# Linear attention behind an adaptive layer norm: the numerators' low parts taken by VectorE straight from the PSUM banks

## The chip, the cores and the metric

The kernel runs on one core of a Trainium2 chip. The metric is the device time of one execution in microseconds (us). The engines are named as in the profile: PE is TensorE (PEld its weight loads), DVE is VectorE, ACT is ScalarE, POOL is GpSimd, SP is the engine whose queue issues most DMAs. A bank is one of the eight 128 x 512 fp32 buffers of PSUM, into which TensorE writes its products.

## The reference

The block takes x (2048 x 640) and a condition vector. Its first half is the attention:

```python
q, k, v = qkv[0], qkv[1], qkv[2]                   # 32 heads of 20
pq = einsum("bhsd,hdf->bhsf", q, w_phi); pk = einsum("bhsd,hdf->bhsf", k, w_phi)
phi_q = concat([softmax(pq), softmax(-pq)]); phi_k = concat([softmax(pk), softmax(-pk)])
kv = einsum("bhsf,bhsd->bhfd", phi_k, v);  z = einsum("bhsf->bhf", phi_k)
num = einsum("bhqf,bhfd->bhqd", phi_q, kv)
den = einsum("bhqf,bhf->bhq", phi_q, z)[..., None] + 1e-6
x = x + ga * ((num / den) @ wo)
```

It is followed by a second modulated layer norm and a two-layer MLP with squared ReLU (640 to 1728 to 640). The change lies in the attention, between num and the product with wo.

## The kernel before, in words

The 2048 rows are 16 tiles of 128, worked on as 8 pairs of tiles. To keep fp32 accuracy, TensorE multiplies in a reduced format (fp32r): each operand is split into a high part (a rounded copy) and a low part (the value less the high part), and a product is three products, high x high, high x low, low x high (`three`). A low part is usually made by `lo`, a VectorE subtraction.

There are three stages. From 0 to about 250 us: the modulation, q, k, v and the sum kv over all rows. From about 250 to 394 us: the attention's tail, where the change lies. From 394 us to the end: the MLP.

Before the tail the exponentials of q are written to DRAM for the first 12 tiles (esp) and read back as el; the last four tiles (12 to 15, `KEPT` = 12) stay on chip, and those of tiles 13, 14, 15 are still made inside the tail: `q_chain` (max, min and two subtractions on VectorE, 13, 14, 15 in j = 1, 3, 5), `exps` (ScalarE), `q_sums` (VectorE). For each tile t the tail then does:

- `e_prod(t)`: VectorE multiplies by z and sums by head (L869, L871); POOL makes the small denominators (L874 to L878).
- `e_recip(t)`, `e_scale(t)`: VectorE inverts them and scales the exponentials; the result is e' (tile ezb, L893 and L898).

For each pair j of tiles:

- `tr_e(j, groups)`: TensorE turns e' by a product with the identity, in six groups of heads (tile te, L913), ScalarE copies each bank out (ept, L915, L917).
- `num(j)`: TensorE multiplies with the block diagonal kv into three banks numa, numb and numc. The first two are used over 512 columns each; numc holds two parts of 256 columns side by side.
- `num_hi(j)`: ScalarE copies the four parts to the high parts of ot (L942).
- `num_lo(j)`: the low parts. TensorE adds minus the identity times the high part into the same banks (L948), so that the bank then holds the low part, and ScalarE copies it out (L951).
- `do_wo(j, i, h, a, b)`: 16 products with wo for tile i of the pair and column block h (384 or 256 columns), tile pwo; ScalarE copies the result to at, and a DMA on its queue writes it to DRAM.

The loop over j runs these skewed: while TensorE does wo of pair j it turns and multiplies pair j + 1, and VectorE makes e' of tiles 2j + 4 and 2j + 5 and the denominators of 2j + 5 and 2j + 6. Each of PE, DVE, ACT and POOL works in the order in which the Python code issues its instructions, since the stage is under a manual schedule; SP's order is set by a planner. In every turn TensorE's order is: wo of tile 2j in two column blocks, wo of tile 2j + 1, first block, with the groups of `tr_e(j + 1)` in between; `num(j + 1)`; 11 products of the last block; the four products with minus identity; the last 5 products. `te_at` says behind which block the two groups of turns stand; for j = 0 (`late_te`) all six stand in one piece ahead of `num(1)`.

The banks of te, numa and numb come from one pool of three that goes round; numc has a bank of its own.

Of the kernel before, what the change touches and what calls it, by code (L numbers as in the profile page):

```python
# [15 lines left out]
P = 128  # L16
# [9 lines left out]
GR = [(120 * g, 120) for g in range(5)] + [(600, 40)]  # L26
NG = len(GR)
# [8 lines left out]
KEPT = NT - POSTPONED  # L36
W2_AT = 48
PLAIN = 2
LAST = 3
W_AT = (  # L40
    *range(21),
# [9 lines left out]
def kernel(  # L51
# [34 lines left out]
    def lo(out_lo, full, hi, eng=None):  # L86
        (eng or nc.vector).tensor_tensor(out_lo, full, hi.bitcast(F32), op=ALU.subtract)  # L87
# [377 lines left out]
    def q_chain(t, whole=True):  # L465
        if t < KEPT:
            EQ[t] = tok2(f"q{t % 2}", f"eq{t}")
        e = EQ[t]
        spread(PQ[t], e, f"q{t}")
        if whole:  # L470
            exps(e)
            q_sums(t)
# [238 lines left out]
    for t in range(2, NT - 2):  # L711
        j, i = divmod(t, 2)
# [167 lines left out]
    def e_recip(t):  # L880
        if t >= NT:
            return
        rs = rs_q[:, t].rearrange("p (s h) -> p s h", s=2)
        nc.vector.reciprocal(DD[t], DD[t])
        for s in range(2):
            nc.vector.tensor_tensor(DN[t][:, s], rs[:, 1 - s], DD[t], op=ALU.mult)

    def e_scale(t):
        if t >= NT:
            return  # L890
        dn = DN[t]
        EU[t] = EZB[t % 4]
        nc.vector.tensor_tensor(  # L893
            EU[t][:, :1200].rearrange("p (u s h d) -> p s u h d", s=2, h=3, d=DH),
            ET[t][:, :, :600].rearrange("p s (u h d) -> p s u h d", h=3, d=DH),
            dn[:, :, :30].rearrange("p s (u h) -> p s u h", h=3)[:, :, :, :, None].to_broadcast([P, 2, 10, 3, DH]), op=ALU.mult
        )
        nc.vector.tensor_tensor(  # L898
            EU[t][:, 1200:].rearrange("p (s h d) -> p s h d", s=2, d=DH),
            ET[t][:, :, 600:].rearrange("p s (h d) -> p s h d", d=DH),  # L900
            dn[:, :, 30:, None].to_broadcast([P, 2, 2, DH]), op=ALU.mult
        )

    def tr_e(j, gs):
        for g in gs:
            o, n = GR[g]
            p = bank(f"te{j}_{g}")
            t = EPT[j, g] = feat("s4", f"ept{j}_{g}")
            for i in range(2):
                for c in range(2 if g < 5 else 1):  # L910
                    a = c * 256 + i * P
                    b, m = (2 * o + 120 * c, 120) if g < 5 else (1200, 80)
                    nc.tensor.transpose(p[:m, a : a + P], EU[2 * j + i][:, b : b + m], ident)  # L913
            if g < 5:
                nc.scalar.activation(t[:120], p[:120].rearrange("p (s n) -> p s n", s=2), AF.Copy)  # L915
            else:
                nc.scalar.activation(t[:80, 0], p[:80, :256], AF.Copy)  # L917
# [15 lines left out]
    def num_parts(j):  # L933
        ps, parts = NUM[j], []
        for b, g in ((0, 2), (1, 2), (2, 1)):
            t = OT[j][:, 2 * b : 2 * b + g]
            parts.append((ps[b][:, : 256 * g].rearrange("p (g n) -> p g n", n=256), t[:, :, 0], t[:, :, 1]))
        return parts + [(ps[2][:120, 256:], OT[j, 5][:120], OT[j, 5][:120])]
# [4 lines left out]

    def num_lo(j):

        for b, (src, hi, _) in enumerate(num_parts(j)):
            r = 120 if b == 3 else P
            nc.tensor.matmul(src, neg[:r, :r], hi, start=False, stop=True, skip_group_check=True)  # L948
        for b, (src, _, low) in enumerate(num_parts(j)):
            r = GR[5][1] if b == 3 else P  # L950
            nc.scalar.activation(low[:r], src[:r], AF.Copy)  # L951
# [3 lines left out]
    def do_wo(j, i, h, a=0, b=16):  # L955
        t = 2 * j + i
        if h == 0 and a == 0:
            PWO[t] = pj(f"pwo{t}")
            AT[t] = row("s2", f"at{t}")
        s = slice(i * P, (i + 1) * P)  # L960
        cs_, n = slice(*CUT[h]), CUT[h][1] - CUT[h][0]
        terms = []
        for g in range(5):
            w, o = WO[g], OT[j]
            terms += three(o[:, g, 0, s], o[:, g, 1, s], w[:, 0, cs_], w[:, 1, cs_])
        terms.append((OT[j, 5][:120, s], WO[5][:120, 0, cs_]))
        mm(PWO[t][h][:, :n], terms[a:b], first=(a == 0), last=(b == 16))
        if b == 16:
            nc.scalar.activation(AT[t][:, cs_], PWO[t][h][:, :n], AF.Copy)
            if h:  # L970
                nc.scalar.dma_start(A1[t], AT[t])
# [83 lines left out]
    def load_xx(j):  # L1055
        if j:
            XX[j] = [row("s2" if j <= PLAIN else "s1", f"xx{j}_{i}") for i in range(2)]
        else:
# [62 lines left out]
    SPREAD, SUMS = {1: 1, 3: 2}, {2: 1, 4: 2}  # L1121
    ln0 = None
    for j in range(NB):
        nxt = j + 1 < NB
        b, c = 2 * j + 5, 2 * j + 6
        late_te = j == 0
        te_at = (0, 1) if 0 < j < 6 else (1, 2)
        if j == 4:
            load_x1(0)
        if j < 5:  # L1130
            p_load()
        if j != 5:
            e_prod(b)
        e_recip(b - 1)
        e_scale(b - 1)
        if j == 5:
            q_chain(KEPT + 3, False)
            add_x(0, 0, 1)
            nc.vector.tensor_tensor(bb, b2s[0], gb_b, op=ALU.mult)
            ln0 = ln_parts(XM[0], "b0")  # L1140
        load_e(b + 2)
        def te(at):
            for i, gs in enumerate((range(3), range(3, NG))):
                if nxt and not late_te and te_at[i] == at:
                    tr_e(j + 1, gs)

        do_wo(j, 0, 0)
        te(0)
        if j == 5:
            exps(EQ[KEPT + 3])  # L1150
            q_sums(KEPT + 3)
            e_prod(b)
        do_wo(j, 0, 1)
        if j == 7:
            t2(0, 0)
            t2(0, 1)
        te(1)
        if j == 5 or j == 6:
            next(ln0)
        if j in SUMS:  # L1160
            q_sums(KEPT + SUMS[j])
        e_prod(c)
        e_recip(b)
        e_scale(b)
        if j in SPREAD:
            q_chain(KEPT + SPREAD[j], False)
        do_wo(j, 1, 0)
        if j == 7:
            t2(0, 2)
            t2(0, 3)  # L1170
        te(2)
        if nxt:
            if late_te:
                tr_e(j + 1, range(NG))
            num(j + 1)
            num_hi(j + 1)
        do_wo(j, 1, 1, 0, 8)
        if j == 7:
            t2(0, 4)
        if not nxt:  # L1180
            do_wo(j, 1, 1, 8, 16)
        if nxt:
            do_wo(j, 1, 1, 8, 11)
            num_lo(j + 1)
            do_wo(j, 1, 1, 11, 16)
        if j in SPREAD:
            exps(EQ[KEPT + SPREAD[j]])
        load_e(c + 2)
        if j == 5:
            next(ln0)  # L1190
        if 1 <= j < 6:
            p_hi()
        if j == 5:
            p_lo(4)
            p_load(4)
        if j == 6:
            p_hi(4)
            p_lo(5)
            p_load(3)
        if j == 7:  # L1200
            p_load(2)
# [16 lines left out]
    def up(j, f):  # L1218

        n, k = FS[f], f % 2  # L1220
        p = UP2[:, :256] if k and j < PLAIN else UP[:, 256 * k : 256 * k + 256]
        terms = []
        for d in range(NC):
            if n == P:
                terms += three(W1[f][:, 0, d], W1[f][:, 1, d], H2[j][:, d, 0], H2[j][:, d, 1])
            else:
                terms += [(W1[f][:, 0, d], H2[j][:, d, 0]), (W1[f][:, 0, d], H2[j][:, d, 1])]
        mm(p, terms, first=(k == 0 or j < PLAIN), skip=True)
        if k == 0:
# [13 lines left out]
    def plain(j, n):  # L1243
        return j < PLAIN or n == NF // 2 - 1 or j == NB - 1 and n >= NF // 2 - LAST

# [6 lines left out]
    def split_a(j, n, parts=(0, 1)):  # L1252
        t = FT[j, n]
        if 0 in parts:
            tag = "rs" if j < PLAIN and (NP * j + n) % 2 or (j, n) == (NB - 1, NP - 1) else "ra"
            RA[j, n] = p3.tile([P, 2, 4, P], F32, tag=tag, name=f"ra{j}_{n}").bitcast(F32R)
# [27 lines left out]
    TD = [{r: dram.tile([P, 2, m], F32, name=f"td{n}_{r}") for r, m in RINGS.items()} for n in range(NP - 1)]  # L1284
    ITEMS = [(j, n, r) for j in range(PLAIN, NB) for n in range(NP) if not plain(j, n) for r in RINGS]
    L, R = slice(0, 384), slice(384, 640)
# [88 lines left out]
    def down_pair(j, n, part):  # L1375
        v, w = W2[2 * n], W2[2 * n + 1]
        last = n == (NF // 2 - 2 if j < NB - 1 else NF // 2 - 1 - LAST)
        if part:
# [127 lines left out]
    for j in range(NB):  # L1506
# [5 lines left out]
        for n in range(NP):  # L1512
# [46 lines left out]
            if j == NB - 1 and n == 1:  # L1559
                for k in range(NP - LAST, NP - 1):  # L1560
                    plain_load(k)
            if j == NB - 1 and n == 3:
                for k in range(NP - LAST, NP - 1):
                    plain_split(k)
# [100 lines left out]
```

## Time and profile before

| | us |
|---|---|
| median of 3 runs | 773.87 (773.56 to 774.21) |
| the profiled execution | 773.97 |
| its span, first to last instruction | 772.2 |
| PE busy | 764.6 (99%) |
| DVE busy | 580.3 (75%) |
| ACT busy | 443.3 (57%) |
| POOL busy | 145.5 (19%) |
| 276 to 394.4 us: PE, DVE, ACT busy | 118.30, 88.58, 75.53 of 118.40 |

A line of the order of time has its start, its duration, the engine, the line of the kernel, the operation, the tile written and the tiles read, the shapes and how many instructions are merged in it; in brackets how long the engine stood idle before it and what ended that. A line of the groups has the busy time, then the mean duration of one in ns, then the idle time before. A line of the stretches has, for each engine, its busy microseconds and in brackets its instructions, then TensorE's granted clock, the share of the DMA engines and GB/s. Durations of consecutive instructions on VectorE and ScalarE overlap by some tens of ns, so what one instruction costs its engine is the distance of starts.

### The profile page before, as it was taken

The numbers are of one execution on the slowest core, as the hardware profiler recorded it, in microseconds if no ns is written. First come the engines' busy times: TensorE is split into PE (matmuls) and PEld (weight loads), VectorE is DVE, ScalarE is ACT, GpSimd is POOL, SyncE is SP. The second block draws the span as 40 slices with busy tenths as digits, with TensorE's granted clock in tenths as the row PEclk, the third lists the DMA queues.
The fourth block names the chain that finished last, engine by engine and source line by source line (L and its number), as shares of the span: only waits on it lengthen the run. The fifth ranks groups of instructions, "written<-read, shape, count | busy, mean of one in ns | idle before, by whom it ended". The sixth has DMA issues, their size and how long they took to land.

```text
span 772.2 us, 15334 instructions
## 1 busy us (share of the span) xinstructions
PE 764.6 (99%) x5989; PEld 744.1 (96%) x5989; DVE 580.3 (75%) x1057; ACT 443.3 (57%) x995; POOL 145.5 (19%) x301
## 2 busy tenths in 40 slices
PE   9999999999999999999999999999999999999997
PEld 9999999999999979998999999999999999999997
DVE  6598897968999899976266666767767566685666
ACT  5766756667853355656776647456463645546331
POOL 3001101202000255631001001122221313213110
PEclk9999999999999999999999999999999999999999
DMA  9711431512333354232247465997666758667460
GB/s 332 297 65 73 137 103 54 186 37 101 133 103 109 111 160 157 86 105 101 91 137 251 137 212 215 292 320 234 202 178 213 231 178 264 198 185 208 128 171 35
DMA packets 50552, 126.03 MB, mean 163 GB/s; under 512 B 5992, under 2 KB 6760, under 8 KB 50480
## 3 DMA queue, kind: packets, MB, share of 16 engines
q1 hardware_dynamic: 33144, 83.99, 31.7%
q0 software_dynamic: 14752, 35.76, 16.7%
q10 hardware_dynamic: 2583, 5.30, 1.8%
q8 instruction: 47, 0.77, 0.4%
q14 instruction: 26, 0.20, 0.1%
HBM read 95.05 MB, written 29.88 MB: 162 GB/s over the span
## 4 chain that ended last, share of the span: by engine, by line
PE 94%; ACT 2%; DVE 1%; DMA 1%; issue 1%; POOL 0%; SPq 0%; ACTq 0%; POOLq 0%
PE up L77 24%; PE acc L77 17%; PE pwo L77 10%; PE pk L77 8%; PE pq L77 8%; PE pv L77 8%; PE acc3x L77 5%; PE kvp L449 2%; PE te L913 2%; PE tb L356 1%; PE numa L77 1%; PE numb L77 1%; PE numc L77 1%; PE ta L356 1%; PE foldk L279 1%; PE foldq L279 1%
## 5 line engine op out<-in xcount | busy, mean ns | idle before, releaser
L77 PE MATMUL up<-h,w 128*128 128x256 f32 x1640 | 206.5, 278 | 0.2 <-ACT ft L1235 0.2
L77 PEld LDWEIGHTS up<-h,w 128*128 128x128 f32 x1640 | 196.1, 188 | 0.3 <-ACT ft L1235 0.3
L1235 ACT ACTIVATE ft<-up,b_t 128x256 f32<-128x256 f32 x104 | 48.8, 469 | 113.9 <-PE up L77 113.4
L77 PE MATMUL acc<-w,ra 128*128 128x384 f32 x452 | 97.9, 335 | 0.0
L1236 DVE TENSOR_TENSOR ft<-ft 128x256 f32<-128x256 f32 x104 | 44.0, 424 | 50.9 <-ACT ft L1235 49.2
L77 PE MATMUL pwo<-wo,ot 128*128 128x256 f32 (+3 forms) x512 | 81.3, 312 | 0.0
L77 PEld LDWEIGHTS pwo<-wo,ot 128*128 128x128 f32 (+1 forms) x512 | 74.9, 188 | 3.0 <-issue 2.7
L77 PE MATMUL pq<-wq,hT 128*128 128x384 f32 (+1 forms) x480 | 75.4, 312 | 0.0
L77 PEld LDWEIGHTS acc<-w,ra 128*128 128x128 f32 x452 | 72.6, 188 | 0.7 <-DVE ra L87 0.5
L77 PE MATMUL pk<-wk,hT 128*128 128x384 f32 (+1 forms) x480 | 72.7, 308 | 0.0
L77 PEld LDWEIGHTS pq<-wq,hT 128*128 128x128 f32 x480 | 71.2, 188 | 0.8 <-issue 0.2
L77 PE MATMUL pv<-wv,hT 128*128 128x384 f32 (+1 forms) x480 | 71.8, 307 | 0.0
L77 PEld LDWEIGHTS pk<-wk,hT 128*128 128x128 f32 x480 | 70.5, 188 | 0.4 <-issue 0.2
L77 PEld LDWEIGHTS pv<-wv,hT 128*128 128x128 f32 x480 | 70.0, 188 | 0.2
L87 DVE TENSOR_TENSOR ra<-ft,ra 128x384 fp32r<-128x384 f32 (+2 forms) x86 | 36.8, 449 | 32.9 <-ACT ra L1259 20.2
L77 PE MATMUL acc3x<-w,ra 128*128 128x256 f32 x248 | 42.4, 278 | 0.0
L1259 ACT ACTIVATE ra<-ft 128x384 fp32r<-128x384 f32 x48 | 25.2, 525 | 28.4 <-DVE ft L1236 22.4
L1345 POOL DMA_DIRECT2D ring_a<-td_a x34 | 18.2, 536 | 123.6 <-PE acc L77 99.6
L77 PEld LDWEIGHTS acc3x<-w,ra 128*128 128x128 f32 x248 | 39.8, 188 | 0.2 <-DVE ra L87 0.2
L1250 DVE TENSOR_TENSOR ft<-ft 128x128 f32<-128x128 f32 x136 | 33.3, 285 | 1.2
L440 DVE TENSOR_REDUCE sk<-ek 128x64 f32<-128x1280 f32 x16 | 23.7, 1483 | 13.9 <-ACT ek L435 13.4
L477 DVE TENSOR_REDUCE rs_q<-eq 128x64 f32<-128x1280 f32 x16 | 23.7, 1479 | 9.6 <-ACT eq L436 9.6
(260 smaller groups left out, 1413.7 us busy)
## 6 DMA issues: line engine op xcount, KB each, us to landing
ring_c<-td_c POOLq DMA_DIRECT2D x34, 384.0 KB, 4.0
ring_a<-td_a POOLq DMA_DIRECT2D x34, 384.0 KB, 3.9
ring_b<-td_b POOLq DMA_DIRECT2D x34, 256.0 KB, 3.9
esp<-eq SPq DMA_DIRECT2D x12, 640.0 KB, 3.1
el<-esp SPq DMA_DIRECT2D x12, 640.0 KB, 5.0
rw<-in_w SPq DMA_DIRECT2D x23, 320.0 KB, 3.6
wm<-in_w_mod SPq DMA_DIRECT2D x20, 320.0 KB, 3.4
xb<-in_x SPq DMA_DIRECT2D x8, 640.0 KB, 4.0
```

What stands on the lines that cost most here:

```text
L77: nc.tensor.matmul(o, a, b, start=first and i == 0, stop=last and i == len(terms) - 1, skip_group_check=skip,)
L87: (eng or nc.vector).tensor_tensor(out_lo, full, hi.bitcast(F32), op=ALU.subtract)
L279: nc.tensor.matmul(p[g // 3][:, (g % 3) * 120 : (g % 3) * 120 + n], r, bd_t[:120, g * 120 : g * 120 + n], start=True, stop=True,)
L356: nc.tensor.transpose(p[:, i * P : (i + 1) * P], xn[:, i, d * P : (d + 1) * P], ident)
L440: nc.vector.tensor_reduce(s, heads(flat(e)), axis=AX.X, op=ALU.add)
L449: nc.tensor.matmul(kvp[g // 4][64 * c : 64 * c + 64, a : a + 2 * n].rearrange("p (s n) -> p s n", s=2), v[:, u], e[:, :, o : o + n], start ...
L477: nc.vector.tensor_reduce(s, heads(flat(e)), axis=AX.X, op=ALU.add)
L1235: nc.scalar.activation(r, p, AF.Relu, bias=b1_t[:, f : f + 1])
L1236: nc.vector.tensor_tensor(r, r, r, op=ALU.mult)
L1250: nc.vector.tensor_tensor(t[:, o], t[:, a], t[:, b], op=op)
L1259: nc.scalar.activation(a[:, 0, :3], t[:, :3], AF.Copy)
L1345: nc.gpsimd.dma_start(RING[j, n, r], TD[n][r].bitcast(F32R))
```

## The change

From the third pair on (j >= 2, `DIRECT`), `num_lo` issues no product with minus identity and no copy by ScalarE. VectorE subtracts the high part from the bank and writes the low part, four subtractions a pair. The first two pairs keep the old way. Beside that, the six groups of turns of pair 1 stand in two pieces, as in j = 6, and two pieces of VectorE's order move: in j = 1, `q_chain(13)` stands behind `num_lo(2)` and not ahead of it; in j = 5, `e_recip(15)` and `e_scale(15)` stand behind `num_lo(6)`. In j = 3, `q_chain(14)` stays where it was.

```diff
+DIRECT = 2
     def num_lo(j):
+        if j >= DIRECT:
+            for b, (src, hi, low) in enumerate(num_parts(j)):
+                r = GR[5][1] if b == 3 else P
+                lo(low[:r], src[:r], hi[:r])
+            return
         for b, (src, hi, _) in enumerate(num_parts(j)):
...
-        late_te = j == 0
         te_at = (0, 1) if 0 < j < 6 else (1, 2)
...
-                if nxt and not late_te and te_at[i] == at:
+                if nxt and te_at[i] == at:
                     tr_e(j + 1, gs)
...
         e_prod(c)
-        e_recip(b)
-        e_scale(b)
-        if j in SPREAD:
+        if j != 5:
+            e_recip(b)
+            e_scale(b)
+        if j == 3:
             q_chain(KEPT + SPREAD[j], False)
         do_wo(j, 1, 0)
...
         if nxt:
-            if late_te:
-                tr_e(j + 1, range(NG))
             num(j + 1)
             num_hi(j + 1)
...
             num_lo(j + 1)
             do_wo(j, 1, 1, 11, 16)
+        if j == 1:
+            q_chain(KEPT + SPREAD[j], False)
+        if j == 5:
+            e_recip(b)
+            e_scale(b)
         if j in SPREAD:
             exps(EQ[KEPT + SPREAD[j]])
```

## The prediction

> **What bounds the kernel now.** I read first the head of the page, then the busy time by stretch inside the attention tail, then the order of time on each engine there.
>
> ```profile
> span 772.2 us, 15334 instructions
> PE 764.6 (99%) x5989; PEld 744.1 (96%) x5989; DVE 580.3 (75%) x1057; ACT 443.3 (57%) x995; POOL 145.5 (19%) x301
> ```
>
> ```profile
> core 0: us, PE busy (x) PEld busy (x) DVE busy (x) ACT busy (x) POOL busy (x), PEclk, DMA share, GB/s
> 275.90:291.67 15.77, 15.70 (x117) 13.71 (x116) 15.42 (x22) 8.38 (x19) 7.59 (x16) 1.00 0.53 168
> 307.05:322.44 15.39, 15.39 (x117) 13.90 (x116) 14.94 (x21) 9.67 (x22) 7.56 (x16) 1.00 0.25 87
> 322.44:337.83 15.39, 15.39 (x117) 13.90 (x116) 14.52 (x20) 8.61 (x20) 7.46 (x13) 1.00 0.26 86
> 368.60:384.00 15.40, 15.37 (x117) 13.87 (x116) 2.57 (x4) 11.93 (x26) 1.29 (x3) 1.00 0.31 106
> ```
>
> The windows are single turns of the loop over j (j = 0, 2, 3, 6). TensorE is busy for all of 15.39 us at a granted clock of 1.00; so what it no longer has to do is time won. But VectorE is busy 14.94 and 14.52 us of j = 2 and 3, only 0.4 to 0.9 us less, and it is the engine that gets the new work. In j = 6 it has 2.57 us: the average over the stage hides where it is short.
>
> **The change, part by part.**
>
> *1. TensorE loses the product with minus identity* (j + 1 = 2 to 7, six pairs). TensorE in order of time:
>
> ```profile
> 304.40 1.53 PE L77 MATMUL pwo<-wo,ot 128*128 128x256 f32 x11
> 305.77 0.39 PE L948 MATMUL numa<-ot,neg 128*128 128x512 f32 x1
> ...
> 306.46 3.52 PE L77 MATMUL pwo<-wo,ot 128*128 128x256 f32 x21
> ```
>
> From the first of the four (here pair 2, in j = 1) to the next pwo product: 306.46 - 305.77 = 0.69 us. Six times 0.69 = 4.14 us off the path.
>
> *2. The first pair's turning in two groups* (tr_e(1) in j = 0).
>
> ```profile
> 275.90 7.79 PE L77 MATMUL pwo<-wo,ot 128*128 128x384 f32 x48
> 283.52 2.68 PE L913 MATMUL te<-ident,ezb 128*120 128x128 f32 x22
> 286.28 1.08 PE L77 MATMUL numa<-ept,kvd 120*64 120x256 f32 x8
> ...
> 373.22 1.47 PE L913 MATMUL te<-ident,ezb 128*120 128x128 f32 x12
> 374.45 3.03 PE L77 MATMUL pwo<-wo,ot 128*128 128x384 f32 x16
> 377.32 1.25 PE L913 MATMUL te<-ident,ezb 128*120 128x128 f32 x10
> 378.60 1.08 PE L77 MATMUL numa<-ept,kvd 120*64 120x256 f32 x8
> ```
>
> In one piece, the 22 turns hold TensorE for 286.28 - 283.52 = 2.76 us, because they run into banks that ScalarE still has to copy out. j = 6 already has the two groups that j = 0 gets: 1.23 + 1.28 = 2.51 us. Gain 0.25 us. The first group now comes two thirds of the way through the 48 products, near 281.0; the last e' that it turns is ready at 279.02 + 0.23 = 279.25:
>
> ```profile
> 279.02 0.23 DVE L898 TENSOR_TENSOR ezb<-el,dn 128x80 f32<-128x80 f32 x1
> ```
>
> so 1.7 us of cover; without it TensorE would wait by the shortfall.
>
> *3. ScalarE loses four copies a pair* (L951, about 1.8 us busy). Nothing gained: TensorE isn't waiting for ScalarE at these places. The copies that remain behind them only come earlier.
>
> *4. VectorE gets four subtractions a pair,* two of 128x512 and two 256 wide, from a bank. No row has 512 from a bank; the nearest, 360 and 256 wide from a bank and 512 from SBUF, with starts of consecutive ones:
>
> ```profile
> L87 DVE TENSOR_TENSOR wk<-foldk,wk 128x360 fp32r<-128x360 f32 x5 | 2.6, 521 | 2.8 <-ACT wk L286 2.8
> L1400 DVE TENSOR_TENSOR y<-y,acc3x 128x256 f32<-128x256 f32 x10 | 4.1, 413 | 0.0
> ```
>
> ```profile
> 504.00 0.69 DVE L87 TENSOR_TENSOR rs<-ft,rs 128x512 fp32r<-128x512 f32 x1
> 504.61 0.42 DVE L1312 TENSOR_TENSOR traw<-traw 128x256 f32<-128x256 f32 x1
> 504.94 0.42 DVE L1312 TENSOR_TENSOR tst_end<-traw,traw 128x256 f32<-128x256 f32 x1
> ```
>
> A 256 wide one from a bank takes 413 ns, from SBUF 0.42 us: the bank costs nothing extra. Starts follow each other by 0.61 and 0.33 us. So 2 x 0.61 + 2 x 0.33 = 1.88 us a pair (upper end, durations laid end to end: 2 x 0.69 + 2 x 0.42 = 2.22).
>
> [...]
>
> *5. Is VectorE in time?* It works in written order, so num_lo(j + 1) stands behind all that is written ahead of it, and the chain runs from num_lo to num_lo:
>
> ```profile
> 303.00 0.59 ACT L942 ACTIVATE ot<-numa 128x512 fp32r<-128x512 f32 x1
> 303.65 0.60 ACT L942 ACTIVATE ot<-numb 128x512 fp32r<-128x512 f32 x1
> 304.51 0.66 ACT L942 ACTIVATE ot<-numc 128x256 fp32r<-128x256 f32 x2 [0.27 <-PE numc L77]
> ```
>
> ```profile
> 303.16 0.81 DVE L429 TENSOR_REDUCE mxq<-eq 128x32 f32<-128x640 f32 x1
> ...
> 306.33 1.48 DVE L869 TENSOR_TENSOR scr<-el,zb 128x1280 f32<-128x1280 f32 x1
> ...
> 318.20 1.48 DVE L869 TENSOR_TENSOR scr<-el,zb 128x1280 f32<-128x1280 f32 x1
> ...
> 331.91 1.49 DVE L869 TENSOR_TENSOR scr<-eq,zb 128x1280 f32<-128x1280 f32 x1
> ```
>
> Pair 2: VectorE is free at 303.16, the copies (0.25 earlier) end at 303.34, 304.0, 304.6, 304.9, so num_lo(2) ends near 305.3 and q_chain(13), moved behind it, starts 2.15 us later than before; its 3.17 us (306.33 - 303.16) follow. TensorE needs the first low part as the weights of the third product of j = 2, near 306.2: no wait.
>
> Pair 3: num_lo(3) takes the place of the row at 318.20, at 318.20 + 2.15 = 320.35; first part done 0.69 later, 321.04. Needed: sixteen products 384 wide take 377.32 - 374.45 = 2.87 us, 0.18 each, so those 256 wide 0.12. Behind the removed group come five of 0.12 and two of 0.18, and weights load about one 0.18 ahead: 0.75 us. Before, that was 306.46 + 15.39 (one turn) + 0.75 = 322.60, now 0.25 + 2 x 0.69 earlier, 320.97. A touch, 0.07 us.
>
> Pair 4: num_lo(4) at 331.91 + 2.15 + 1.88 = 335.94; first part done 336.63. Needed: 322.60 + 15.39 - 0.25 - 3 x 0.69 = 335.67. TensorE waits 0.96, say 1.0 us with the hand-over; this contains pair 3's 0.07. Its later parts follow faster (0.61) than TensorE needs them (six products, 1.06).
>
> Pair 5: what is between num_lo(4) and num_lo(5) is what stood from 306.33 to 318.20 (two tiles and a q_sums), 11.87 us. num_lo(5) at 335.94 + 1.88 + 11.87 = 349.7, first part 350.4; needed 322.60 + 2 x 15.39 - 0.25 - 4 x 0.69 + 1.0 = 351.4. In time by 1.0. For pairs 6 and 7 the load falls (2.57 us in j = 6): no wait.
>
> *6. The moves.* q_chain(13) (four VectorE instructions) issues no DMA. Behind it wait ScalarE's exps(13), and in its queue the copy of the next W1 rows and the copies of turned e':
>
> ```profile
> 277.81 25.77 SPq L859 DMA_DIRECT2D el<-esp  x6
> ```
>
> ```profile
> 308.47 0.74 ACT L435 ACTIVATE eq<-eq 128x640 f32<-128x640 f32 x1 [0.40 <-ACT at L969]
> ...
> 310.74 1.56 ACT L915 ACTIVATE ept<-te 120x512 f32<-120x512 f32 x3
> ```
>
> ```profile
> 313.03 1.26 PE L913 MATMUL te<-ident,ezb 128*120 128x128 f32 x10
> ```
>
> q_chain ends near 308.55, so exps starts at 308.6 where ScalarE could have begun at 307.5, 0.94 earlier than now; the ept copies start 0.1 to 0.2 later than now, near 310.9, done 311.4 for the first. TensorE's next group wants that bank near 312.1 (313.03 less 0.94). Cover 0.6 us; cost nothing. In j = 5, e_recip(15) and e_scale(15) go behind num_lo(6): they then end near 368 and are turned at 373.22 - 2.7 = 370.5. No DMA is in either; SP's loads of el wait for e_scale and would shift with it, but all six are issued by 277.81 + 25.77 = 303.6, ahead of the delay. POOL's little chains start behind e_prod, whose order is unchanged. Cost nothing.
>
> **Sum.** -4.14 - 0.25 + 1.0 = -3.4 us on the profiled execution, 773.97 (span 772.2 and 1.8 around it): 770.6. The median of the runs shown is 0.10 lower, so 770.5.
>
> Unknown ends: VectorE's price of 2.22 instead of 1.88 delays pairs 2, 3 and the first part of 4 by some 0.8, the price of the shared bank (next) 0.3: 771.6. With the wait gone, and with each removed group taking along the gap before it (305.77 - 304.40 less 11 x 0.12 = 0.05, six times 0.3): 769.2, and I go to 769.0.
>
> [...]
>
> **Rivals.**
>
> *No wait shows.* VectorE turns out as much as 1.0 us faster over the chain, or TensorE's need comes later than I count. For it: VectorE's gaps include 0.05 to 0.1 us between dependent instructions that may close. Against it: the rows from 303.16 to 331.91 show no idle time at all to close up. Time: 769.5.
>
> *VectorE becomes the bound, and the kernel is slower.* Place: num_lo(3) to num_lo(5). Work between two num_lo: 3.17 + 11.87 = 15.04 us, then 13.71, then 11.87, against a turn of 15.39 - 0.69 = 14.70 us. Each us more per num_lo delays the end by about 2.3 us at pair 4 and by one more at pair 5 once its 1.0 of cover is gone. The gain of 3.4 us is used up at 1.88 + 3.4 / 2.3 = 3.4 us a pair, 1.8 times the rows; at 4.2 us (a 512 wide part at 1.35) the time would be some 776. For it: VectorE is 97% busy in j = 2. Against it: no subtraction in the trace is that dear.
>
> *The gain is given back.* Something I cost at nothing, such as ScalarE held by exps(13) with te and num behind it, takes 2 to 4 us. Point of decision: 0.6 us of cover there. Time: 772.5 to 774.
>
> **How the numbers follow.** Forecast (VectorE late by about 1 us, 769.9 to 771.7): 0.70. No wait: 0.13, 769.5. Given back: 0.10, of which 0.02 still under 772.3. Slower: 0.07. A measurement of this kernel tells about 0.2%, 1.55 us: faster is under 772.3, slower over 775.4. Faster 0.70 + 0.13 + 0.02 = 0.85, same 0.08, slower 0.07. The range takes the forecast, the lower end of no wait and the smaller part of given back: 769.0 to 772.6.
>
> **What would show it.** Right: no products from neg after pair 1; the turn j = 2 to 4 at 14.7 us but for one with about 1 us in which TensorE's weights wait for a VectorE subtraction, at pair 4; 512 wide subtractions near 0.69 us; VectorE with no idle time from 276 to 350; numa of pair 1 at 286.0. Wrong: a wait at pair 2 or at pair 5 and 6, subtractions over 0.8 us, te waiting for ept copies in j = 2, or a stage behind 394 us that doesn't start 3 us earlier.

## The result, and the profile after

| | before | changed |
|---|---|---|
| median of 5 runs each, us | 773.66 (773.54 to 774.21) | 770.42 (769.86 to 770.89) |
| ratio, 95% interval | | 0.9956 (0.9943 to 0.9969) |
| span of the profiled execution, us | 772.2 | 768.7 |
| first product with wo to first product of the MLP, us | 118.48 | 115.07 |

The kernel is 0.44% faster, and the interval leaves out 1. In what follows "the stage" is the last row: from the first pwo product to the first up product, 275.90 to 394.38 before, 275.38 to 390.45 now, 3.41 us shorter. What lies ahead of it and behind it is the same code; it differs by 0.5 us either way, and cancels. The stage's last end before, and both ends now:

```profile
394.38 3.81 PE L77 MATMUL up<-h,w 128*128 128x256 f32 x32
```

```profile
275.38 5.01 PE L78 MATMUL pwo<-wo,ot 128*128 128x384 f32 x32
...
390.45 4.72 PE L78 MATMUL up<-h,w 128*128 128x256 f32 x40
```

The head of the page, changed kernel:

```profile
span 768.7 us, 15287 instructions
PE 760.7 (99%) x5965; PEld 740.3 (96%) x5965; DVE 591.4 (77%) x1081; ACT 434.8 (57%) x971; POOL 146.8 (19%) x301
```

TensorE has 24 instructions fewer (six pairs of four), VectorE 24 more. A group of turns is a row of te, in which TensorE turns e'; a turn of the loop is one j. TensorE in order of time, the first group of turns in j = 1 to 6 and the wait at pair 4:

```profile
293.83 1.47 PE L914 MATMUL te<-ident,ezb 128*120 128x128 f32 x12
...
303.79 4.88 PE L78 MATMUL pwo<-wo,ot 128*128 128x256 f32 x32
308.51 1.47 PE L914 MATMUL te<-ident,ezb 128*120 128x128 f32 x12
...
323.45 1.48 PE L914 MATMUL te<-ident,ezb 128*120 128x128 f32 x12
...
333.41 2.46 PE L78 MATMUL pwo<-wo,ot 128*128 128x256 f32 x18
336.25 2.72 PE L78 MATMUL pwo<-wo,ot 128*128 128x384 f32 x14 [0.38 <-DVE ot L88]
338.81 1.47 PE L914 MATMUL te<-ident,ezb 128*120 128x128 f32 x12
...
353.49 1.48 PE L914 MATMUL te<-ident,ezb 128*120 128x128 f32 x12
...
370.00 1.47 PE L914 MATMUL te<-ident,ezb 128*120 128x128 f32 x12
```

From one of these groups to the next: 14.68, 14.94, 15.36 us, then 14.68 again, where it was 15.39 (in j = 6 the group stands one block later, so the last distance is longer). The 11 + 5 products around the removed group now run through with the next block as one row of 32. Two turns of the loop are longer than 14.68, by 0.26 and 0.68: there TensorE's weight loads wait for a low part, at the third product of pair 3 and of pair 4:

```profile
320.89 2.39 PEld L78 LDWEIGHTS pwo<-wo,ot 128*128 128x128 f32 x14 [0.29 <-DVE ot L88]
...
336.25 2.39 PEld L78 LDWEIGHTS pwo<-wo,ot 128*128 128x128 f32 x14 [0.70 <-DVE ot L88]
```

VectorE's order of time, the first subtraction of pairs 2 to 6 and what is around the first of them:

```profile
303.02 0.69 DVE L88 TENSOR_TENSOR ot<-numa,ot 128x512 fp32r<-128x512 f32 x1 [0.30 <-ACT ot L943]
303.67 0.69 DVE L88 TENSOR_TENSOR ot<-numb,ot 128x512 fp32r<-128x512 f32 x1
304.60 0.75 DVE L88 TENSOR_TENSOR ot<-numc,ot 128x256 fp32r<-128x256 f32 x2 [0.24 <-ACT ot L943]
305.27 0.80 DVE L430 TENSOR_REDUCE mxq<-eq 128x32 f32<-128x640 f32 x1
...
320.16 0.68 DVE L88 TENSOR_TENSOR ot<-numa,ot 128x512 fp32r<-128x512 f32 x1
...
322.02 1.47 DVE L870 TENSOR_TENSOR scr<-el,zb 128x1280 f32<-128x1280 f32 x1
...
335.51 0.68 DVE L88 TENSOR_TENSOR ot<-numa,ot 128x512 fp32r<-128x512 f32 x1
...
349.08 0.68 DVE L88 TENSOR_TENSOR ot<-numa,ot 128x512 fp32r<-128x512 f32 x1
...
364.10 0.69 DVE L88 TENSOR_TENSOR ot<-numa,ot 128x512 fp32r<-128x512 f32 x1 [1.22 <-ACT ot L943]
```

At pair 2 VectorE is early and waits for ScalarE's copies (0.30 and 0.24), at pairs 3, 4 and 5 no row has a bracket: VectorE comes late, not the copies. At pair 6 it waits again (1.22). A full num_lo takes 322.02 - 320.16 = 1.86 us.

### The profile page after: what moved, and what is told of

Read it like the earlier page. It is cut to its first block, busy times and chain, and to the rows that moved or that the text cites. A ratio compares the mean times of both kernels' runs of the same rounds, so it can differ in the third digit from the quotient of the medians.

```text
span 768.7 us, 15287 instructions
## 1 busy us (share of the span) xinstructions
PE 760.7 (99%) x5965; PEld 740.3 (96%) x5965; DVE 591.4 (77%) x1081; ACT 434.8 (57%) x971; POOL 146.8 (19%) x301
## 4 chain that ended last, share of the span: by engine, by line
PE 90%; DVE 4%; ACT 3%; DMA 1%; issue 1%; POOL 1%; SPq 0%; DVEq 0%; POOLq 0%; ACTq 0%
PE up L78 24%; PE acc L78 18%; PE pwo L78 10%; PE pk L78 7%; PE pq L78 7%; PE pv L78 6%; PE acc3x L78 5%; PE te L914 3%; PE kvp L450 2%; PE tb L357 1%; PE numa L78 1%; PE numb L78 1%; PE numc L78 1%; DMA wm<-in_w_mod 1%; PE foldk L280 1%
## 5 line engine op out<-in xcount | busy, mean ns | idle before, releaser
L1244 ACT ACTIVATE ft<-up,b_t 128x256 f32<-128x256 f32 x104 | 48.8, 469 | 114.1 <-PE up L78 113.5
L878 POOL TENSOR_TENSOR dn<-dn,rs_q 128x32 f32<-128x32 f32 x32 | 22.6, 706 | 66.6 <-DVE dn L872 66.3
```

Of the source, the lines that this page charges most:

```text
L878: nc.gpsimd.tensor_tensor(dn[:, s], dn[:, s], rs[:, 1 - s], op=ALU.mult)
L1244: nc.scalar.activation(r, p, AF.Relu, bias=b1_t[:, f : f + 1])
```

## The experiments

Each run is the changed kernel with the edit shown, except where the kernel before is named. The times of before that it is compared with were taken on the same chip.

Two theories stand against each other. The chain: VectorE's work from about 276 us to pair 4 is one unbroken chain, and the point at which it ends sets TensorE's delay, wherever in the chain a piece stands. The rival: each wait is a price at its own place, and moving a piece behind a num_lo saves it.

**1. q_chain(13) back ahead of num_lo(2).**

```diff
-        if j == 3:
+        if j in SPREAD:
             q_chain(KEPT + SPREAD[j], False)
         do_wo(j, 1, 0)
...
-        if j == 1:
-            q_chain(KEPT + SPREAD[j], False)
```

> The changed kernel with one move undone: q_chain(13) stands ahead of num_lo(2) again. Theory (VectorE's work from 276 us to pair 4 is one unbroken chain, and the end of that chain sets TensorE's delay): TensorE waits about 0.65 us at pair 2 (first low part done near 306.5, needed near 305.9), but VectorE no longer waits for ScalarE's copies at pair 2, reaches pair 4 some 0.8 us earlier, and the waits at pairs 3 and 4 (0.26 and 0.68 us in the changed kernel) go: stage from the first product with wo to the first of the MLP about 114.8 us against 115.07, time about 770.1. Rival (each wait is a price of its own, so the move pays): the 0.65 us come on top of the 0.94, stage 115.7, time about 771.1.

Measured: 770.32 us, ratio to before 0.9950 (0.9936 to 0.9963); stage 114.71 us. The only weight load that waits for a low part is at pair 2:

```profile
307.17 2.37 PEld L78 LDWEIGHTS pwo<-wo,ot 128*128 128x128 f32 x14 [0.61 <-DVE ot L88]
```

The waits at pairs 3 and 4 are gone, as the chain has it: the stage is 0.36 us shorter than with the move, where the rival has it 0.6 longer. VectorE no longer waits for ScalarE's copies at pair 2, which were 0.54 us in the changed kernel, and measured from the stage's start it begins num_lo(4) 0.78 us earlier. This move of the change costs the stage 0.36 us. In the time, 0.1 us, it can't be told.

**2. e_recip(15) and e_scale(15) back ahead of num_lo(6).**

```diff
-        if j != 5:
-            e_recip(b)
-            e_scale(b)
+        e_recip(b)
+        e_scale(b)
...
-        if j == 5:
-            e_recip(b)
-            e_scale(b)
```

> The changed kernel with the other move undone: e_recip(15) and e_scale(15) stand ahead of num_lo(6) again. Theory: VectorE must wait for POOL (364.1 us) and scale (to 366.2) ahead of num_lo(6); first low part done near 367.0, needed near 365.5: a new wait of about 1.5 us at pair 6, stage about 116.6 us, time about 771.9. Rival (VectorE has slack from j = 5 on, so the place is all one): no wait, 770.4.

Measured: 772.09 us, ratio 0.9975 (0.9966 to 0.9984); stage 116.56. The weight loads that wait for VectorE, pairs 3, 4 and 6:

```profile
321.38 2.38 PEld L78 LDWEIGHTS pwo<-wo,ot 128*128 128x128 f32 x14 [0.29 <-DVE ot L88]
...
336.75 2.42 PEld L78 LDWEIGHTS pwo<-wo,ot 128*128 128x128 f32 x14 [0.73 <-DVE ot L88]
...
367.57 4.33 PEld L78 LDWEIGHTS pwo<-wo,ot 128*128 128x128 f32 x30 [1.55 <-DVE ot L88]
```

The first two are those of the changed kernel, the third is new: this move is worth 1.5 us. Ahead of num_lo(6) VectorE stands idle until POOL has made the denominators of tile 15, and then scales, up to 366.84:

```profile
364.64 0.35 DVE L885 RECIPROCAL dd<-dd 128x32 f32<-128x32 f32 x1 [1.24 <-POOL dd L879]
```

In the changed kernel that idle time lies ahead of num_lo(6) too, where VectorE waits for the copies (1.22 us at 364.10), and the scaling behind it follows without a wait. The piece moved isn't needed until the turns of pair 7, and VectorE has idle time behind it; q_chain(13) is followed by a chain without any up to pair 6.

**3. Each of the first three subtractions twice.**

```diff
-                lo(low[:r], src[:r], hi[:r])
+                for _ in range(1 if b == 3 else 2):
+                    lo(low[:r], src[:r], hi[:r])
```

> The changed kernel with each of the first three subtractions of a pair made twice (same result), 1.53 us more on VectorE for each of six pairs. Theory (VectorE is the bound through j = 2 to 5): waits of about 2.0 us at pair 3, 2.2 at pair 4, 0.5 at pair 5, 0.6 at pair 6, together 5.2 in place of 0.94; stage about 119.3 us, time about 774.7, no better than before the change. Rival (VectorE at 77% of the span has room, its slack takes the work up): within 0.5 us of 770.4. A rival in between (only the wait of the one late pair grows, by the 1.5): 772.

Measured: 776.32 us, ratio 1.0031 (1.0020 to 1.0043), slower than before the change; stage 121.38, more than either theory had. VectorE in order of time, the first (doubled) subtraction of pairs 2 to 5, and what follows at pairs 2 and 3:

```profile
302.70 1.42 DVE L88 TENSOR_TENSOR ot<-numa,ot 128x512 fp32r<-128x512 f32 x2 [0.34 <-ACT ot L943]
304.03 1.41 DVE L88 TENSOR_TENSOR ot<-numb,ot 128x512 fp32r<-128x512 f32 x2
...
321.37 1.41 DVE L88 TENSOR_TENSOR ot<-numa,ot 128x512 fp32r<-128x512 f32 x2
...
325.13 1.48 DVE L870 TENSOR_TENSOR scr<-el,zb 128x1280 f32<-128x1280 f32 x1
...
338.62 1.41 DVE L88 TENSOR_TENSOR ot<-numa,ot 128x512 fp32r<-128x512 f32 x2
...
354.11 1.40 DVE L88 TENSOR_TENSOR ot<-numa,ot 128x512 fp32r<-128x512 f32 x2
```

The expectation was off in the price of the repeat. Two subtractions into the same place take 304.03 - 302.70 = 1.33 us, not 2 x 0.61. Less the 0.60 from one to the next that writes another place, that leaves about 0.73 for the second, an estimate: no less than the 0.68 that one lasts in the changed kernel. A num_lo is 325.13 - 321.37 = 3.76 us, 1.90 more instead of 1.53. The chain itself is as expected: measured from the stage's start (0.36 us earlier in this run), VectorE reaches pairs 3, 4 and 5 later by 1.57, 3.47 and 5.39 us, each step one more price of a num_lo. The stage is 6.31 us longer. Where, is told by the first groups of turns in j = 2 to 6 (the row of 375.87 is that of j = 6):

```profile
308.19 1.47 PE L914 MATMUL te<-ident,ezb 128*120 128x128 f32 x12
...
325.67 1.48 PE L914 MATMUL te<-ident,ezb 128*120 128x128 f32 x12
...
342.92 1.48 PE L914 MATMUL te<-ident,ezb 128*120 128x128 f32 x12
...
358.41 1.47 PE L914 MATMUL te<-ident,ezb 128*120 128x128 f32 x12
...
375.87 1.47 PE L914 MATMUL te<-ident,ezb 128*120 128x128 f32 x12
```

Against the distances in the changed kernel the turns with pairs 3 and 4 are longer by 2.54 and 1.89, together 4.43 us, that with pair 5 by 0.81 and that with pair 6 by 0.95. Two covers broke on the way. q_chain(13) now ends so late that ScalarE's exps(13) holds the copies of turned e', and TensorE waits in j = 2,

```profile
312.66 1.39 PE L914 MATMUL te<-ident,ezb 128*120 128x128 f32 x10 [1.11 <-ACT ept L916]
```

the place at which the prediction gave 0.6 us of cover. And at pair 6 exps(15) holds the copies in the same way, so that the products of num(6) wait 0.41 us for them.

**4. q_chain(14) behind num_lo(4) too.**

```diff
-        if j == 3:
-            q_chain(KEPT + SPREAD[j], False)
...
-        if j == 1:
+        if j in SPREAD:
             q_chain(KEPT + SPREAD[j], False)
```

> The changed kernel with q_chain(14) moved behind num_lo(4), as q_chain(13) already stands behind num_lo(2). Theory: the wait at pair 4 goes (VectorE reaches num_lo(4) at 332.3, before ScalarE's copies are done), that at pair 3 (0.26) stays; but VectorE now waits for the copies at pair 4 and is 0.7 us later at pair 5, where about 0.3 us of wait appears. Stage about 114.7 us, time about 770.1. Rival (the wait of pair 4 is a price of its own): all of 0.68 won, stage 114.4, time 769.7.

Measured: 770.28 us, ratio 0.9951 (0.9939 to 0.9964); stage 114.67. Waits for VectorE at pairs 3 and 5:

```profile
321.49 2.38 PEld L78 LDWEIGHTS pwo<-wo,ot 128*128 128x128 f32 x14 [0.30 <-DVE ot L88]
...
351.08 2.39 PEld L78 LDWEIGHTS pwo<-wo,ot 128*128 128x128 f32 x14 [0.31 <-DVE ot L88]
```

Of the 0.70 us at pair 4 about half comes back one pair later, as the chain has it; the rival had 114.4.

**5. Beside that, q_sums(13) behind num_lo(3).**

```diff
-        if j in SUMS:
+        if j == 4:
             q_sums(KEPT + SUMS[j])
...
+        if j == 2:
+            q_sums(KEPT + SUMS[j])
```

> The changed kernel with q_chain(14) behind num_lo(4) and q_sums(13) behind num_lo(3). Theory: no wait at pairs 3 and 4; about 0.3 us left at pair 5, because the chain of VectorE's work up to there is as long as before. Stage about 114.4 us, time about 769.8. Rival (each wait is a price of its own): all 0.94 won, stage 114.1.

Measured: 769.80 us, ratio 0.9945 (0.9931 to 0.9959); stage 114.38, with one wait left at pair 5, 0.29 us. Again the chain's number and not the rival's 114.1.

**6. Only what must stands ahead of a num_lo.** On top of run 5:

```diff
+        if j == 5:
+            q_chain(KEPT + 3, False)
         e_recip(b - 1)
         e_scale(b - 1)
         if j == 5:
-            q_chain(KEPT + 3, False)
             add_x(0, 0, 1)
-            nc.vector.tensor_tensor(bb, b2s[0], gb_b, op=ALU.mult)
...
-        if j == 4:
-            q_sums(KEPT + SUMS[j])
-        e_prod(c)
+        if j != 4:
+            e_prod(c)
         if j != 5:
             e_recip(b)
             e_scale(b)
+        if j == 4:
+            q_sums(KEPT + SUMS[j])
...
+        if j == 4:
+            e_prod(c)
         if j == 5:
             e_recip(b)
             e_scale(b)
+            nc.vector.tensor_tensor(bb, b2s[0], gb_b, op=ALU.mult)
```

> As the run before, and in j = 4 and 5 only as much of VectorE's work ahead of a num_lo as must be: e_prod(14) behind num_lo(5), q_chain(15) ahead of e_recip(14), the bias product behind num_lo(6). Theory: no wait for a low part at any pair; stage 114.1 us, time about 769.5, the most that is to be had from the order of VectorE's work. Rival (some other cover breaks, such as POOL's denominators for tile 13 or 14 or the turned e' of pair 7): a new wait of 0.3 to 1 us in j = 4 to 6, stage 114.4 to 115.1.

Measured: 769.58 us, ratio 0.9945 (0.9933 to 0.9958); stage 114.15. No weight load waits for VectorE in the stage, and j = 1 to 4 are alike, 14.67, 14.67, 14.66 and 14.67 us; the third, which was 15.36:

```profile
323.60 1.47 PE L914 MATMUL te<-ident,ezb 128*120 128x128 f32 x12
...
338.26 1.48 PE L914 MATMUL te<-ident,ezb 128*120 128x128 f32 x12
```

**7. The changed and the reordered kernel side by side,** on one chip.

> The changed kernel itself, for comparison on the same chip as the next run: 770.4 us, stage 115.1 us.

> The reordered kernel once more beside the changed one: both theories that tell it apart by TensorE's waits expect 0.9 us less than the changed kernel, near 769.5, stage 114.15 us. If the stage's gain is lost again in the MLP behind it, the two times agree within 0.3 us.

Measured: 770.40 us (770.02 to 771.00), ratio 0.9954 (0.9942 to 0.9967), stage 115.11; and 770.33 us (769.02 to 770.37), ratio 0.9944 (0.9931 to 0.9958), stage 114.26. The stage is 0.85 us shorter again. The median of the time isn't: the five runs of the reordered kernel lie at 769.0 to 769.2 and at 770.3 to 770.4, and such steps, whose cause is open, hide 0.9 us. The MLP behind takes 377.9 us in both, so nothing is given back there; ahead of the stage the reordered kernel's profiled execution is 0.20 us later. That the reordered kernel is the faster of the two is shown by its stage, not by its time.

**8. The second pair by VectorE as well.**

```diff
-DIRECT = 2
+DIRECT = 1
```

> The changed kernel with the second pair (pair 1) subtracted by VectorE too. Theory (VectorE has no room at all from 276 us on): num_lo(1) stands behind e_scale(5), which ends at 292.2, first part done 292.9, needed near 290.5: a wait of 2.4 us against 0.69 us saved, and the 1.86 us go down VectorE's whole chain to pair 4; stage about 116.8 us, time about 772.1. Rival (one more pair saves one more 0.69): 769.7.

Measured: 771.41 us, ratio 0.9973 (0.9962 to 0.9983); stage 116.62. The new wait, at pair 1; those at pairs 3 and 4 stay at 0.29 and 0.70:

```profile
292.62 2.39 PEld L78 LDWEIGHTS pwo<-wo,ot 128*128 128x128 f32 x14 [2.26 <-DVE ot L88]
```

One more pair costs 1.5 us of stage instead of saving 0.7: there is no room on VectorE that early. But the 1.86 us more on VectorE don't add to its lateness at pair 4, as was expected. TensorE has been held up as well, and at pair 2 VectorE again waits for the copies:

```profile
304.37 0.69 DVE L88 TENSOR_TENSOR ot<-numa,ot 128x512 fp32r<-128x512 f32 x1 [0.22 <-ACT ot L943]
```

So the chain that ends at pair 4 is not unbroken from 276 us: it starts at the copies of pair 2.

**9. The two groups of turns alone,** an edit of the kernel before:

```diff
-        late_te = j == 0
...
-                if nxt and not late_te and te_at[i] == at:
+                if nxt and te_at[i] == at:
...
-            if late_te:
-                tr_e(j + 1, range(NG))
```

> The kernel before with one part of the change alone: the first pair's turning in two groups. Theory: TensorE's turn j = 0 gets 0.25 us shorter and nothing else moves; stage 118.2 us against 118.48, time 773.4 to 773.6, which timing alone cannot tell. Rival (the first group comes before e' of tile 3 is there, or the gain is taken back by a later wait): stage unchanged or longer.

Measured: 774.01 us, ratio 1.0004 (0.9995 to 1.0012), no difference; stage 118.45, 0.03 us shorter and not 0.25. TensorE in j = 0:

```profile
276.27 5.03 PE L77 MATMUL pwo<-wo,ot 128*128 128x384 f32 x32
281.14 1.47 PE L913 MATMUL te<-ident,ezb 128*120 128x128 f32 x12
282.37 3.08 PE L77 MATMUL pwo<-wo,ot 128*128 128x384 f32 x16
285.29 1.25 PE L913 MATMUL te<-ident,ezb 128*120 128x128 f32 x10
286.58 1.08 PE L77 MATMUL numa<-ept,kvd 120*64 120x256 f32 x8
```

The turns themselves take 1.23 + 1.29 = 2.52 us, 0.24 less than in one piece, as predicted. But the 48 products beside them, 7.62 us in one piece, take 4.87 + 2.92 = 7.79 when they are cut. TensorE reaches num(1) 0.07 us earlier (0.10 in the changed kernel), and of that 0.03 is left at the end of the stage.

## Why the prediction was right, point by point

Time 770.42 for 770.5; the stage gains 3.41 us for 3.4. The mechanism held: TensorE's gain of about 0.7 us a pair, less VectorE's lateness at pair 4. That the sum agrees so closely is luck: the products won 0.12 us more than put, the two groups of turns 0.15 to 0.22 less, and the wait cost 0.06 less.

- *Step 1, the product with minus identity, 0.69 each.* Right in mechanism, a little small: a turn without waits is 14.68 us for 15.39, so 0.71 each, 4.26 in all for 4.14. The gap of 0.05 ahead of the group, which the prediction kept for its lower end only, may go with it in part; the turns of run 9, whose products stand as before, already lie at 15.37 and 15.38, so 0.02 can't be told.
- *Step 2, the turns in two groups, 0.25.* Wrong in size: 0.07 to 0.10 at num(1), and 0.03 at the end of run 9. The step compared the lengths of the groups only and left out what cutting the block of products costs, 0.17 us in run 9. Its cover held: no turn waited for e'.
- *Step 3, ScalarE's copies.* Their going alone won nothing that shows: in run 6 the six groups and run 9's 0.03 account for 4.29 of the 4.33 us gained.
- *Step 4, VectorE's price, 1.88 a pair.* Measured 1.86, and 0.67 to 0.69 us for 512 columns from a bank, where 0.69 was taken from a row with SBUF operands; the rows show no difference between the two kinds of source.
- *Step 5, VectorE in time?* Which pairs wait is right. num_lo(3), (4) and (5) were put at 320.35, 335.94 and 349.7 and began at 320.16, 335.51 and 349.08 in a stage that itself began 0.52 earlier: 0.33 and 0.09 later and 0.1 earlier than put. No wait at pairs 2, 5 and 6; a touch at pair 3 (0.07 predicted, 0.26 measured) and in all 0.96 predicted, 0.94 measured. That these two agree is in part luck. At pair 2 VectorE came through 0.48 us later than put, where it waited twice for copies (0.30 and 0.24; the sign "no idle time from 276 to 350" did not hold). By pair 4 it had made up 0.39, mostly because the same pieces took less time than before: 13.49 us for 13.71 between num_lo(3) and num_lo(4). TensorE, which won less in j = 0, needed the part 0.1 later. And the 0.75 us from the removed group to the first load add up to 0.78 by their own terms.
- *Step 6, the moves at no cost.* exps(13) did wait for VectorE, 2.24 us, and no copy behind it came too late; run 3 shows what happens without the cover. That pair 6 needs the move of e_scale(15), and not only the lighter load, wasn't in the prediction; run 2 gives its price, 1.5 us. That the move of q_chain(13) costs 0.36 us of stage was not in it either (run 1).
- *The bank shared by two parts, 0.3 in the prediction's upper end.* No run shows a price of the bank: none has the parts in two banks. What the runs show is a wait. At pair 2 the first copy of numc, 0.38 us long from 303.91, ended at 304.29, but the third subtraction began at 304.60, when the second copy was through:

```profile
303.91 0.66 ACT L943 ACTIVATE ot<-numc 128x256 fp32r<-128x256 f32 x2 [0.27 <-PE numc L78]
```

  In run 6, where VectorE is early at pairs 4 and 5 as well, the third subtraction waits for ScalarE there too, 0.23 us each time. Why it starts behind the second copy and not behind the first isn't shown. The 0.31 us from 304.29 to 304.60 fall into the chain at pair 2, and the prediction had its 0.3 as an upper end, not in its sum.
- *The rivals.* "No wait shows" is what run 6 makes of the kernel by reordering: 0.9 us of stage. "VectorE becomes the bound" is what run 3 makes of it: slower than before, at a num_lo of 3.76 us, where the prediction put the point of no gain at 3.4. Its 2.3 us of delay for each us give 4.4 us up to pair 4 for the 1.90; measured 4.43. Beyond the 1.0 us of cover at pair 5 it has 0.9 more; measured 0.81. The 0.95 at pair 6 it did not have, so the gain is used up sooner: a straight line through the stages of the two kernels meets that of before at a num_lo of about 2.9 us, an estimate. Its "some 776" for 4.2 us leaves out the share of pair 5, 1.3 us by its own terms. "The gain is given back" did not come: no group of turns in j = 2 waits for ScalarE, and the MLP starts 3.93 us earlier, 3.41 of it from the stage.

## What to carry to other kernels

Before work goes from the engine that bounds a stage to another, follow that other engine from one due point to the next: here VectorE was busy 75% of the span, but 94 to 98% of j = 0, 2 and 3, and its lateness added up from pair to pair up to pair 4, behind which it has less to do than a turn lasts (13.57 us from num_lo(4) to num_lo(5), for 14.68). Moving a piece of work behind a due point helps as far as the due points behind it have time to spare. It won 1.5 us for e_scale(15), with idle time behind it, and 0.40 for q_chain(14), half of whose wait came back one pair later; it lost 0.36 for q_chain(13), whose place was then idle and whose work made the next pairs late. And instructions that were put into the middle of a block of products lengthened that block by 0.17 us here (run 9), which took most of a gain of 0.24.

## What the runs showed of the hardware that was not expected

A VectorE subtraction of 128x512 followed another one by 0.60 us where they wrote different places (pairs 3, 4 and 5 of the changed kernel), and by about 0.73, an estimate, where it wrote the same place again (the 1.33 of run 3 less the 0.60 to the next; the second one also reads the same operands). A block of 48 products on TensorE took 0.17 us longer (7.79 for 7.62, run 9) with 12 transposes put behind its first 32, and 0.14 in the changed kernel (4.84 + 2.92).
